# Attention with sinks and windows, then a leaky-ReLU MLP: sinks' loads, the order of the first copies, and GpSimd for the sinks of chunk 0

## The chip, the cores and the metric

The kernel runs on one core of a Trainium2 chip. Its engines are TensorE (PE), VectorE (DVE), ScalarE (ACT), GpSimd (POOL) and SyncE (SP); each runs its own instructions in order, and they wait for one another by semaphores. The metric is the device time of one execution in microseconds, lower is better.

## What is computed

Four batches of 8 heads, 768 positions, head size 64. Heads 0, 2 and 6 ("retrieval") attend to all earlier positions; heads 1, 3, 4, 5 and 7 ("streaming") only to the first 4 positions (the sinks) and to the last 64. The result, 3072 tokens of 512, goes through two matrices with a leaky ReLU between them.

```python
scores = scale * np.matmul(q, k.transpose(0, 1, 3, 2))
stream_keep = causal & (is_sink | in_win)
scores = np.where(mask, scores, -1e9)          # causal, or stream_keep for streaming heads
a = np.exp(scores - max); a = a / a.sum(-1)
x = (a @ v) as [B * S, H * D]
h = x @ w_in                                    # 512 -> 2048
g = np.maximum(0.01 * h, h)
out = g @ w_out                                 # 2048 -> 512
```

## The kernel before

The tokens are cut into 8 chunks of 384: chunk n is half c = n % 2 of batch b = n // 2. For each chunk the kernel brings q and k into the layout with the head size across the partitions (`qt`, `kt`), computes scores per head into PSUM, exponentiates them on ScalarE into `at` (retrieval) or `ats` (streaming), multiplies by v into the accumulator `po` of each pair of heads, divides by the sums (`finish`, L499 and L501, giving `xs`), transposes to `xt` (`x_t`, L512 and L515) and runs the MLP (L562 for w_in, L570 for the leaky ReLU, L602 for w_out). The order on each engine is that of the program text: nothing is reordered, and the program interleaves attention of one chunk with the MLP of another by hand (`slots`, `merge`).

Chunk 0 is special, since there is nothing to run beside it. Its k is loaded in float32 in two halves by SP (`load_k0`, tile `f`) and cast by DVE and ACT (`kb`, L312, L313). Its q is loaded and cast by one DMA of POOL (`load_q0`, L80). `prep_first` transposes both on TensorE (L324, L329) and empties the results from PSUM: `k_rows(half, hh)` (L341 on DVE, L339 on ACT) for heads 2p + hh of two pairs p, `q_rows(half)` (L355 on DVE, L357 on ACT). Filler matmuls (`warm_up`, L200) lie between. Two masks are added to the scores of chunk 0 by TensorE: `n_caus` (L423) and, for streaming heads, `n_win0` (L463), which `negative_window` (L178, L179) makes on DVE.

The sinks are handled apart. `sv` holds the first 4 rows of v of each head and batch (L650: five small DMAs on ACT's queue, one for each streaming head and all batches). `sink_values` (L187, L189) spreads them into `vs`, one column block to a head, with the 0/1 mask `m_h`; `sink_keys` (L238) copies the sinks' columns of `kt` into `ksink`; `sink` computes all sinks' scores at once (L396, then the exponential at L399), and `finish` adds `vs` times these to the accumulators. `sink_after` says after which heads the sinks' slot comes. `v_shift_pe` (L224, L227) makes `vb`, v moved by 64 rows, for the first two tiles; later chunks do it by DMA (`v_shift`, L215, L216).

POOL issues nearly all loads, in program order, each after the one eight before it has landed: for chunk 0 q, v (`va`, L97) and the first two quarters of w_in (L103), then k, q and v of chunk 1 (`kb`, `qb`, `va`), the other quarters of w_in and those of w_out (L106), and four memsets of `kz` (L674, L675). Chunk 1's k and q are transposed at L272, after the first seven groups of the MLP of chunk 0.

Of the kernel before, what the change touches and what calls it, by code (L numbers as in the profile page):

```python
# [13 lines left out]
ACTF = mybir.ActivationFunctionType  # L14
ALU = mybir.AluOpType

IS_RETR = [1, 0, 1, 0, 0, 0, 1, 0]
# [4 lines left out]
def kernel(  # L22
# [12 lines left out]
    nc = tc.nc  # L35
    B, H, S, D = q.shape
    assert (B, H, S, D) == (4, 8, 768, 64)
    NS = int(n_sink)
# [43 lines left out]
    def load(n, nms="kqv"):  # L82

        b, c = divmod(n, 2)
        for nm in nms:
            if nm == "k" and n >= BY_DMA:

                for g in range(3):
                    for hh in range(2):
                        nc.gpsimd.dma_start(out=kz[n % 2][:, g, hh::2, D * hh : D * hh + D],  # L90
                                            in_=nat[nm][b, c, :, hh::2, g])
                continue
            if nm != "v":
                cast[nm, n] = rot.tile([128, 3, H, D], BF16, name=f"{nm}b", tag=f"{nm}b", bufs=2)
            for g in range(3):
                o = va[b % 2][:, 3 * c + g, :, 0:D] if nm == "v" else cast[nm, n][:, g]
                nc.gpsimd.dma_start(out=o, in_=nat[nm][b, c, :, :, g])  # L97

    def load_w(which, i):

        if which == "in":
            c = slice(512 * i, 512 * i + 512)
            nc.gpsimd.dma_start(out=w_in_bf[:, :, c], in_=w_in_r[:, :, c])  # L103
        else:
            c = slice(4 * i, 4 * i + 4)
            nc.gpsimd.dma_start(out=w_out_bf[:, c, :], in_=w_out_r[:, c, :])  # L106
# [12 lines left out]
    kt = [bf(f"kt{i}", 4, 2, S) for i in range(2)]  # L119
    va = [bf(f"va{i}", 6, H, D + 1) for i in range(2)]  # L120
    vb = [bf(f"vb{i}", 5, H, D + 1) for i in range(2)]
    vs = [bf(f"vs{i}", H, D + 1) for i in range(2)]

    sv = one.tile([128, B, D], FP32, name="sv")
# [21 lines left out]
    m_h = bf("m_h", H)  # L146
# [9 lines left out]
    def spread(ap, n, w):  # L156
        return ap.rearrange("p (o r) -> p o r", o=1).to_broadcast([128, n, w])

    def shifts():

        nc.vector.tensor_copy(shift[:, 0, 0:64], ident[:, 64:128])
        nc.vector.tensor_copy(shift[:, 1, 64:128], ident[:, 0:64])

    def masks_sinks():

        with nc.allow_low_precision("one term of each sum is not zero"):
            nc.vector.tensor_reduce(m_h[:], ident[:, 0 : NS * H].rearrange("p (h r) -> p h r", r=NS),
                                    axis=mybir.AxisListType.X, op=ALU.add)
        for h in range(H):
            if IS_RETR[h]:  # L170
                nc.vector.memset(m_h[:, h : h + 1], 0.0)
# [11 lines left out]
        nc.vector.tensor_copy(m_win0[:, 0, :], m_caus[:, 0:64])  # L183
        nc.vector.memset(m_win0[0:NS, 1, :], 1.0)

    def sink_values(b):
        nc.vector.tensor_copy(vs[b % 2][:, :, D], m_h[:])  # L187
        m = m_h[:, 1:H].rearrange("p (h o) -> p h o", o=1).to_broadcast([128, H - 1, D])
        nc.vector.tensor_tensor(vs[b % 2][:, 1:H, 0:D], spread(sv[:, b, :], H - 1, D), m, op=ALU.mult)  # L189


    idle = {}
# [1 line left out]
    def warm_up(n, w=128):  # L194
        if not idle:
            idle["s"] = bf("idle", 512)
            nc.vector.memset(idle["s"][:], 0.0)
            idle["d"] = bank("psS", [128, 512], FP32)
        for _ in range(n):
            nc.tensor.matmul(idle["d"][:, 0:w], lhsT=idle["s"][:, 0:128], rhs=idle["s"][:, 0:w], start=True, stop=True)  # L200
# [9 lines left out]
    def v_shift(n, eng=None):  # L210
        eng = eng or nc.scalar
        b, c = divmod(n, 2)
        i = b % 2
        lo, hi = (0, 2) if c == 0 else (2, 5)
        eng.dma_start(out=vb[i][0:64, lo:hi], in_=va[i][64:128, lo:hi])  # L215
        eng.dma_start(out=vb[i][64:128, lo:hi], in_=va[i][0:64, lo + 1 : hi + 1])  # L216
# [9 lines left out]
            src = p[:, 0:w].rearrange("p (h d) -> p h d", h=7)  # L226
            nc.vector.tensor_copy(vb[0][:, t, 1:H, :], src)  # L227

    def sink_keys(n):
        b, c = divmod(n, 2)  # L230
        if c:
            return
        for hh in range(2):
            r = slice(64 * hh, 64 * hh + 64)
            d = ksink[b % 2].rearrange("p (a c) -> p a c", a=4)[r, :, NS * hh : NS * hh + NS]
            st = [p for p in range(4) if not IS_RETR[2 * p + hh]]
            for ps2 in [slice(0, 4)] if len(st) == 4 else [slice(p, p + 1) for p in st]:
                nc.vector.tensor_copy(d[:, ps2], kt[b % 2][r, ps2, hh, 0:NS])  # L238

    def prep_pair(n, p, tag="pt", eng=("v", "v", "v")):  # L240
        b, c = divmod(n, 2)
# [66 lines left out]
    def prep_first():  # L308

        k0 = stage["k"].rearrange("p h (g d) -> p g h d", g=3)  # L310
        qts[0] = rot.tile([128, 4, CH], BF16, name="qt", tag="qt", bufs=3)
        nc.vector.tensor_copy(cast["k", 0][:, :, 0:4], k0[:, :, 0:4])  # L312
        nc.scalar.activation(out=cast["k", 0][:, :, 4:8], in_=k0[:, :, 4:8], func=ACTF.Copy)  # L313
        pts = {}
        for nm, half, tag in (("k", 0, "pt"), ("k", 1, "py"), ("q", 0, "po"), ("q", 1, "po")):
            pt = pts[nm, half] = bank(tag, [128, 2, 4, 128], BF16)
            if nm == "q":
                continue
            if half == 1:
                warm_up(9)  # L320
            for e in range(2):
                p = 2 * half + e
                for g in range(3):
                    nc.tensor.transpose(pt[:, e, g, :], cast[nm, 0][:, g, 2 * p : 2 * p + 2, :], ident[:])  # L324
        warm_up(8)
        for p in range(4):
            for g in range(3):
                for hh in range(2):
                    nc.tensor.transpose(pts["q", p // 2][64 * hh : 64 * hh + 64, p % 2, g, :],  # L329
                                        cast["q", 0][:, 2 * p + hh, D * g : D * g + D], ident[:])  # L330
        tok = lambda ap: ap.rearrange("p e (t g) -> p e t g", g=3)

        def k_rows(half, hh, act=False):
            ps2 = slice(2 * half, 2 * half + 2)
            r = slice(64 * hh, 64 * hh + 64)
            src = pts["k", half][r, :, 0:3, :].rearrange("p e g t -> p e t g")
            dst = tok(kt[0][r, ps2, hh, 0:CH])
            if act:
                nc.scalar.activation(out=dst, in_=src, func=ACTF.Copy)  # L339
            else:  # L340
                nc.vector.tensor_copy(dst, src)  # L341

        def q_rows(half):
            return (tok(qts[0][:, 2 * half : 2 * half + 2, :]),
                    pts["q", half][:, :, 0:3, :].rearrange("p e g t -> p e t g"))

        nc.vector.tensor_sub(m_w[:], m_caus[:, 64:128], m_caus[:, 0:64])
        negative_causal()
        k_rows(0, 0)
        k_rows(0, 1)  # L350
        k_rows(1, 0, True)
        k_rows(1, 1, True)
        negative_window()
        d, r = q_rows(0)
        nc.vector.tensor_copy(d, r)  # L355
        d, r = q_rows(1)
        nc.scalar.activation(out=d, in_=r, func=ACTF.Copy)  # L357


    xts = {}  # L360
# [260 lines left out]
    def run(*lists):  # L621
        for l in lists:
            for f in l:
                f()
# [6 lines left out]
    def merge(ms, as_):  # L631

        r, done = [], 0
        for j, m in enumerate(ms):
            want = (j + 1) * len(as_) // len(ms)
            r += as_[done:want] + [m]
            done = want
        return r + as_[done:]
# [6 lines left out]
    make_identity(nc, ident)  # L645
    warm_up(9, 512)
    nc.vector.memset(sv[:], 0.0)
    for h in range(H):
        if not IS_RETR[h]:
            nc.scalar.dma_start(out=sv[NS * h : NS * h + NS], in_=v[:, h, 0:NS, :].rearrange("b r d -> r b d"))  # L650
    for t in va:
        nc.vector.memset(t[:, :, :, D], 1.0)
    nc.vector.memset(shift[:], 0.0)
# [3 lines left out]
    load(0, "v")  # L657
    load_w("in", 0)
    load_w("in", 1)
    load(1, "kq")  # L660
    load(1, "v")
    load_w("in", 2)
    load_w("in", 3)
    for j, a in enumerate(ats):
        if j < 2:
            nc.vector.memset(a[:, :, 1:3, :], 0.0)
        else:
            z = idle["s"][:, 0:CH].rearrange("p (a e t) -> p a e t", a=3, e=2)
            nc.scalar.activation(out=a[:, :, 1:3, :], in_=z, func=ACTF.Copy)
    masks_sinks()  # L670
    for i in range(4):
        load_w("out", i)
    for t in kz:
        nc.gpsimd.memset(t[:, :, 0::2, D:], 0.0)  # L674
        nc.gpsimd.memset(t[:, :, 1::2, 0:D], 0.0)  # L675
    prep_first()
    A0 = Attention(0, ("psS", "ph"), po_tags=("po", "po", "py", "po"))
    a0 = A0.slots(order=[0, 2, 1, 3, 4, 5, 6, 7], lag=lambda t: 4, XLAG=None, sink_after={0, 2})
    warm_up(8)
    run(a0[0:4])  # L680
    sink_keys(0)
    sink_values(0)
    shifts()
    run(a0[4:6])
    v_shift_pe()
    run(a0[6:14])
    i0 = in_first(0, ("ph", "psS", "ph", "psS"))
# [22 lines left out]
    a1 = A1.slots(order=[0, 2, 6, 1, 3, 4, 5, 7], lag=lambda t: max(2, 7 - t // 2))  # L710
    run(a1[0:11])
    v_shift(1, nc.sync)
    run(merge(in0[8:12], a1[11:16]))
    out0 = out_slots(0, ("po", "ph", "py"))
    run(merge(in0[12:16] + out0[0:3], spaced(a1[16:], 9)))
# [72 lines left out]
```

## Time and profile before

| | |
|---|---|
| median of 4 runs | 237.67 us (237.25 to 238.12) |
| the profiled execution | 238.12 us |
| its span, first to last instruction | 236.4 us |
| instructions | 5109 |
| granted TensorE clock | 0.999 of full speed |
| TensorE / ScalarE / VectorE / GpSimd busy | 226.0 / 129.4 / 89.1 / 77.8 us |
| HBM read, written | 27.28 MB, 6.29 MB |

The profiled execution is the slowest of the four. A profile line of the timeline gives start, length, engine, line of the source, operation, output and inputs with shapes, how often; in brackets stands how long the engine was idle before it, and what released it. Matmuls overlap: the length of one is longer than the distance to the next. A line of the chain of waits gives start, length, and what held the end of the program in that time. DMA issues on the engines count as busy on POOL, and the last figure of an issue line is the time from issue to landing.

### The profile page before, as it was taken

To read this page: it belongs to the slowest core of one execution; us is meant where nothing else is said; L and a number is where in the kernel's file an instruction comes from. 1 tells how busy PE (TensorE), PEld (TensorE's weight loads), DVE (VectorE), ACT (ScalarE), POOL (GpSimd) and SP (SyncE) were. 2 spreads that over 40 slices of the span, in tenths; PEclk is the share of its full clock that TensorE was granted. 3 is DMA by queue.
4 is the path that set the end of the run, shared out by engine and by line. 5 is a ranking of instruction groups with operands and counts; after the bars stand their busy time and mean duration, and the time that the engine had idled before them with its cause. 6 is when DMAs were issued, how large, how long until landed. Compare 5 with 4: busy or idle time off the path is not lost.

```text
span 236.4 us, 5109 instructions
## 1 busy us (share of the span) xinstructions
PE 226.0 (96%) x2039; PEld 138.9 (59%) x2064; DVE 89.1 (38%) x244; ACT 129.4 (55%) x282; POOL 77.8 (33%) x102
## 2 busy tenths in 40 slices
PE   6799999999999999999989999999999999999994
PEld 2686666555664677566546665566556665555553
DVE  7754478307762244054211451244212441111121
ACT  4787776661551798756347763556356763433300
POOL 7958932789762263345039200000000000000000
PEclk9999999999999999999999999999999999999999
DMA  7999999999999999999999998495210211111112
GB/s 164 173 183 163 219 222 188 150 127 166 149 130 235 171 182 146 181 137 173 147 173 164 118 170 144 111 136 145 80 44 0 65 45 52 44 44 44 47 44 89
DMA packets 110699, 30.54 MB, mean 129 GB/s; under 512 B 101460, under 2 KB 106836, under 8 KB 110676
## 3 DMA queue, kind: packets, MB, share of 16 engines
q0 software_dynamic: 74144, 13.24, 74.6%
q1 hardware_dynamic: 36432, 16.95, 39.0%
q8 instruction: 16, 0.26, 0.5%
q14 instruction: 7, 0.06, 0.1%
q10 hardware_dynamic: 100, 0.02, 0.0%
HBM read 27.28 MB, written 6.29 MB: 142 GB/s over the span
## 4 chain that ended last, share of the span: by engine, by line
PE 85%; DMA 7%; ACT 3%; DVE 2%; issue 1%; POOLq 0%; ACTq 0%
PE ph L562 26%; PE py L602 14%; PE pt L602 10%; PE po L383 7%; PE psS L562 6%; PE ph L602 4%; PE psS L416 4%; PE psS L602 4%; DMA xt<-xs 4%; DMA q<-in_q_dram 3%; PE psS L458 2%; ACT at L425 2%; PE po L602 1%; PE psS L396 1%; PE ph L416 1%
## 5 line engine op out<-in xcount | busy, mean ns | idle before, releaser
L562 PE MATMUL ph<-xt,w_in_bf 128*128 128x384 bf16 x416 | 85.7, 326 | 0.8 <-DMA xt<-xs 0.6
L570 ACT ACTIVATE g<-ph 128x384 bf16<-128x384 f32 x102 | 50.2, 492 | 51.6 <-PE ph L562 51.3
L562 PEld LDWEIGHTS <-w_in_bf 128*128 128x128 bf16 x512 | 46.5, 98 | 31.4 <-issue 0.5
L602 PEld LDWEIGHTS <-g 128*128 128x128 bf16 x400 | 35.8, 98 | 26.3
L602 PE MATMUL py<-w_out_bf,g 128*128 128x512 bf16 (+1 forms) x164 | 42.5, 368 | 0.6
L425 ACT ACTIVATE at<-psS 128x384 bf16<-128x384 f32 x66 | 32.4, 494 | 11.6 <-PE psS L416 10.2
L90 POOL DMA_DIRECT2D kz<-in_k_dram x30 | 22.4, 768 | 29.5 <-DMA qb<-in_q_dram 12.1
L602 PE MATMUL pt<-w_out_bf,g 128*128 128x512 bf16 x103 | 28.4, 379 | 0.5
L97 POOL DMA_DIRECT2D va<-in_v_dram x24 | 21.1, 896 | 8.1 <-DMA w_out_bf<-in_moe_w_out_dram 3.3
L97 POOL DMA_DIRECT2D qb<-in_q_dram x21 | 18.6, 893 | 13.7 <-DMA va<-in_v_dram 7.6
L416 PE MATMUL psS<-qt,kt 128*128 128x384 bf16 (+2 forms) x86 | 21.5, 288 | 0.2
L562 PE MATMUL psS<-xt,w_in_bf 128*128 128x384 bf16 x96 | 20.5, 326 | 0.0
L383 PE MATMUL po<-va,at 128*128 128x65 bf16 x237 | 19.5, 193 | 0.2 <-DVE at L433 0.2
L383 PEld LDWEIGHTS <-at 128*128 128x128 bf16 x252 | 15.9, 98 | 5.6 <-issue 0.6
L466 ACT ACTIVATE ats<-psS 128x384 bf16<-128x384 f32 x32 | 15.8, 493 | 4.9 <-PE psS L458 4.0
L607 DVE COPY o<-py 128x512 f32<-128x512 f32 (+1 forms) x11 | 7.3, 665 | 28.0 <-PE py L602 28.0
L501 DVE TENSOR_TENSOR xs<-po,linv 128x384 bf16<-128x384 f32 x30 | 16.7, 558 | 1.0
L416 PEld LDWEIGHTS <-kt 128*128 128x128 bf16 x108 | 10.2, 97 | 8.8 <-issue 1.7
L458 PEld LDWEIGHTS <-kt 128*128 128x128 bf16 x240 | 11.8, 98 | 5.5 <-issue 0.2
L433 DVE TENSOR_TENSOR at<-at,m_caus 128x128 bf16<-128x128 bf16 x21 | 4.7, 225 | 26.4 <-ACT at L425 26.4
L383 PEld LDWEIGHTS <-ats 128*128 128x128 bf16 x240 | 11.4, 97 | 3.8 <-DVE ats L476 0.6
L570 ACT ACTIVATE g<-psS 128x384 bf16<-128x384 f32 x22 | 10.8, 492 | 4.7 <-PE psS L562 4.6
(135 smaller groups left out, 241.0 us busy)
## 6 DMA issues: line engine op xcount, KB each, us to landing
out_dram<-o SPq DMA_DIRECT2D x23, 256.0 KB, 2.6
va<-in_v_dram POOLq DMA_DIRECT2D x24, 128.0 KB, 10.8
qb<-in_q_dram POOLq DMA_DIRECT2D x21, 128.0 KB, 10.3
w_in_bf<-in_moe_w_in_dram POOLq DMA_DIRECT2D x4, 512.0 KB, 9.6
w_out_bf<-in_moe_w_out_dram POOLq DMA_DIRECT2D x4, 512.0 KB, 15.7
kz<-in_k_dram POOLq DMA_DIRECT2D x30, 64.0 KB, 7.4
vb<-va SPq DMA_DIRECT2D x8, 195.0 KB, 6.5
vb<-va SPq DMA_DIRECT2D x6, 130.0 KB, 7.9
```

Of the source, the lines that this page charges most:

```text
L90: nc.gpsimd.dma_start(out=kz[n % 2][:, g, hh::2, D * hh : D * hh + D], in_=nat[nm][b, c, :, hh::2, g])
L97: nc.gpsimd.dma_start(out=o, in_=nat[nm][b, c, :, :, g])
L383: nc.tensor.matmul(o, lhsT=lhsT, rhs=rhs, start=first, stop=False, skip_group_check=True)
L416: nc.tensor.matmul(s[:, off : off + w], lhsT=kt[i][:, p, hh, 128 * kj : 128 * kj + 128], rhs=qts[n][:, p, lo:CH], start=(j == 0), stop=(j ...
L425: nc.scalar.activation(out=a[:, 0:off], in_=s[:, 0:off], func=ACTF.Exp, scale=SM)
L458: nc.tensor.matmul(s[:, 64 * m : 64 * m + 64], lhsT=kt[i][:, p, hh, k0 : k0 + 128], rhs=qts[n][:, p, 64 * m : 64 * m + 64], start=(m == 0) ...
L466: nc.scalar.activation(out=av_, in_=s[:, 0:CH].rearrange("p (j e f) -> p j e f", j=3, e=2), func=ACTF.Exp, scale=SM)
L501: nc.vector.tensor_tensor(xs[:], po[:, :, :, 0:D], linv.to_broadcast([128, 3, 2, D]), op=ALU.mult)
L562: nc.tensor.matmul(ph[:, 0:CH], lhsT=w_in_bf[:, g, 128 * t : 128 * t + 128], rhs=xts[n][:, g, :], start=(g == 0), stop=(g == KG - 1))
L570: nc.scalar.activation(out=gs[n][:, t, :], in_=ph[:, 0:CH], func=ACTF.Prelu, alpha=0.01)
L602: nc.tensor.matmul(py[n][:, 0 : c1 - c0], lhsT=gs[n][:, ng, 128 * tt : 128 * tt + 128], rhs=w_out_bf[:, ng, c0:c1], start=(ng == 0), stop= ...
L607: nc.vector.tensor_copy(o[:, 0 : c1 - c0], py[n][:, 0 : c1 - c0])
```

## The change

- `sv` is loaded by one DMA to a batch on SP's queue, all eight heads' sinks in one (`load_sinks`): batch 0 at the start, after the two loads of `f`; batches 1 to 3 after `v_shift(1)`. The retrieval heads' rows are now loaded too; `m_h` makes them zero.
- In `prep_first` the first `q_rows` stands before the second `k_rows` on DVE, and the second `q_rows` goes from ACT to DVE, behind `negative_window`.
- `sink_values(0)` and `sink_keys(0)` run on POOL, and stand before the loads of chunk 1 in POOL's queue; `prep_first` is called before these loads too.
- `shifts()` runs before `prep_first`; three of the five `ats` are cleared by DVE instead of two.
- The sinks' slot of chunk 0 comes after heads 0 to 3 instead of after heads 0 and 2; `v_shift_pe` stays behind slot 5, and so comes ahead of the sinks.
- The eight filler matmuls ahead of chunk 0's scores are gone.

```diff
+    def load_sinks(b):
+        nc.sync.dma_start(out=sv[0 : NS * H, b, :], in_=v[b, :, 0:NS, :])
+
-    def sink_values(b):
-        nc.vector.tensor_copy(vs[b % 2][:, :, D], m_h[:])
+    def sink_values(b, eng=None):
+        eng = eng or nc.vector
+        eng.tensor_copy(vs[b % 2][:, :, D], m_h[:])
...
-        nc.vector.tensor_tensor(vs[b % 2][:, 1:H, 0:D], spread(sv[:, b, :], H - 1, D), m, op=ALU.mult)
+        eng.tensor_tensor(vs[b % 2][:, 1:H, 0:D], spread(sv[:, b, :], H - 1, D), m, op=ALU.mult)
...
-    def sink_keys(n):
+    def sink_keys(n, eng=None):
...
-                nc.vector.tensor_copy(d[:, ps2], kt[b % 2][r, ps2, hh, 0:NS])
+                (eng or nc.vector).tensor_copy(d[:, ps2], kt[b % 2][r, ps2, hh, 0:NS])
...
         k_rows(0, 0)
+        nc.vector.tensor_copy(*q_rows(0))
         k_rows(0, 1)
         k_rows(1, 0, True)
         k_rows(1, 1, True)
         negative_window()
-        d, r = q_rows(0)
-        nc.vector.tensor_copy(d, r)
-        d, r = q_rows(1)
-        nc.scalar.activation(out=d, in_=r, func=ACTF.Copy)
+        nc.vector.tensor_copy(*q_rows(1))
...
     nc.vector.memset(sv[:], 0.0)
-    for h in range(H):
-        if not IS_RETR[h]:
-            nc.scalar.dma_start(out=sv[NS * h : NS * h + NS], in_=v[:, h, 0:NS, :].rearrange("b r d -> r b d"))
+    load_sinks(0)
...
     load_w("in", 1)
-    load(1, "kq")
-    load(1, "v")
-    load_w("in", 2)
-    load_w("in", 3)
     for j, a in enumerate(ats):
-        if j < 2:
+        if j < 3:
...
     masks_sinks()
+    shifts()
+    sink_values(0, nc.gpsimd)
+    prep_first()
+    sink_keys(0, nc.gpsimd)
+    load(1, "kq")
+    load(1, "v")
+    load_w("in", 2)
+    load_w("in", 3)
     for i in range(4):
         load_w("out", i)
...
-    prep_first()
     A0 = Attention(0, ("psS", "ph"), po_tags=("po", "po", "py", "po"))
-    a0 = A0.slots(order=[0, 2, 1, 3, 4, 5, 6, 7], lag=lambda t: 4, XLAG=None, sink_after={0, 2})
-    warm_up(8)
-    run(a0[0:4])
-    sink_keys(0)
-    sink_values(0)
-    shifts()
-    run(a0[4:6])
+    a0 = A0.slots(order=[0, 2, 1, 3, 4, 5, 6, 7], lag=lambda t: 4, XLAG=None, sink_after={0, 1, 2, 3})
+    run(a0[0:6])
     v_shift_pe()
...
     v_shift(1, nc.sync)
+    for b in range(1, B):
+        load_sinks(b)
```

## The prediction

> **What bounds the kernel now.** I read the page first (shares, slices), then the chain of waits, then the timeline of each engine up to 20 us, since the diff touches almost nothing later.
>
> ```profile
> PE 226.0 (96%) x2039; PEld 138.9 (59%) x2064; DVE 89.1 (38%) x244; ACT 129.4 (55%) x282; POOL 77.8 (33%) x102
> PE   6799999999999999999989999999999999999994
> PE 85%; DMA 7%; ACT 3%; DVE 2%; issue 1%; POOLq 0%; ACTq 0%
> ```
>
> TensorE is 96% busy and carries 85% of the chain; what it lacks lies in the first slices. The chain of waits up to 45 us says how it starts (start, length, what):
>
> ```profile
> 1.33 7.70 DMA q<-in_q_dram
> ...
> 9.07 0.55 PE po L329 x12
> ...
> 9.64 0.97 DVE qt L355
> ...
> 10.65 0.32 PE ph L416
> ```
>
> Chunk 0's q lands at 1.33 + 7.70 = 9.03. Twelve transposes and one VectorE copy later the scores begin, at 10.65; from there to 20 us the chain is TensorE alone. A change here is worth what it does to 10.65, plus the stalls that it puts between 10.65 and 20. The timeline of VectorE, then of TensorE:
>
> ```profile
> 6.28 1.94 DVE L341 COPY kt<-pt 64x768 bf16<-64x768 bf16 x2 [0.51 <-PE pt L324]
> 8.25 0.32 DVE L178 TENSOR_SCALAR n_win<-m_w 128x320 bf16<-128x320 bf16 x1
> 8.63 0.09 DVE L179 MEMSET n_win<- 4x32 uint32 x1
> 9.64 0.96 DVE L355 COPY qt<-po 128x768 bf16<-128x768 bf16 x1 [0.92 <-PE po L329]
> 10.51 0.36 DVE L238 COPY ksink<-kt 64x4 bf16<-64x4 bf16 x2
> ...
> 15.22 0.20 DVE L499 RECIPROCAL linv<-po 128x6 f32<-128x6 f32 x1 [0.87 <-PE po L383]
> 15.45 0.56 DVE L501 TENSOR_TENSOR xs<-po,linv 128x384 bf16<-128x384 f32 x1
> ```
>
> ```profile
> 11.63 0.60 PE L396 MATMUL ph<-qt,ksink 128*128 128x256 bf16 x4
> 12.07 0.26 PE L383 MATMUL po<-va,at 128*128 128x65 bf16 x3
> ...
> 16.44 0.33 PE L512 MATMUL pt<-ident,xs 128*128 128x128 bf16 x3
> ```
>
> To be seen: both k copies and the window mask fit before 8.72, in time in which VectorE would wait for q anyway (0.92 us is still left idle).
>
> GpSimd issues the loads of chunk 1 early (timeline), and they land ten us later (DMA issues of the stretch 9 to 10 us, last figure):
>
> ```profile
> 6.01 1.52 POOL L103 DMA_DIRECT2D w_in_bf<-in_moe_w_in_dram x2
> 7.48 2.71 POOL L97 DMA_DIRECT2D kb<-in_k_dram x3
> 10.49 2.71 POOL L97 DMA_DIRECT2D qb<-in_q_dram x3 [0.30 <-DMA va<-in_v_dram]
> kb<-in_k_dram POOLq DMA_DIRECT2D x2, 128.0 KB, 10.1
> ```
>
> [...] kb, issued at 7.48, lands at 17.5, after w_in, issued at 6.01 and 6.77, has landed at 14.1 and 16.7; its ten us are backlog.[...] the one-output MEMSET kz of 768 elements took 0.757 us[...].[...] The trace grants 1.00 in every stretch from 1 to 20 us, with gaps of at most 1.22 us.
>
> **The change, part by part.**
>
> 1. *Sinks' v.* ACT's five issues (1.50 to 3.43) go; its table load, at 3.47, starts some 2 us earlier and its cast of k (6.02) waits for the second half of f (1.29 + 4.3 = 5.6) instead: 0.4 us earlier, for nothing, since q is later. Does q land sooner? In the DMA view the sv queue holds 43 packets at 1.6% of 16 engines from 3 to 6 us and 57 at 2.2% from 6 to 9: 0.8 + 1.1 = 1.8 engine-us[...]; I take 0[...]. Below nothing: the new load is one more behind f on SP, 32 rows of 256 B; under 0.05. The three late loads go on SP behind vb (24.35, 26.18), where nothing follows for several us; sink values of batch 1 come tens of us later.
>
> 2. *Order on VectorE.* One more ats memset (0.21) and the two shift copies (0.09 apart) come before the k cast: 4.63 becomes 4.9 to 5.0, the first k copy ends near 7.65 instead of 7.25, hidden by q at 9.03. Then the first q copy at 9.64, as before: scores still at 10.65. Behind it now stand the second k copy (0.97): 10.52 to 11.49; mask (0.32) to 11.84; its memset to about 11.99; second q copy, from ACT, 11.95 to 12.95.
>
> 3. *Order on TensorE.* The fifth slot was the sinks' scores at 11.63; now it is head 1, whose k comes at 11.5 and whose bank is free at 11.06 + 0.49 = 11.55: no wait. Its six matmuls end at 11.80, then the mask matmul waits for the memset until 12.03: **+0.23**. The sinks' scores move behind v_shift_pe, to about 13.5; second q copy (12.95) is there. ACT has the exponentials in another order; each bank is freed in time.
>
> 4. *Finish.* Pairs 0 and 1 now finish together after the sinks' slot and h6's second score: the first reciprocal goes from 15.22 to about 15.86. Reciprocal and product take 15.45 - 15.22 + 0.56 = 0.79, so the first xs is ready at 16.65 and, with 0.05 to signal, its transposes at 16.70, where TensorE arrives at about 16.6: up to 0.1 more, of which the third part's wait already covers some. The next pairs follow at 0.71 and keep up (xs of pair 2 at 18.07 for 18.25, of pair 3 at 18.78 for 19.06). By my walk the first w_in matmul goes from 17.35 to 17.60: **+0.25** for parts 3 and 4 together.
>
> 5. *GpSimd.* After 7.5: vs copy (0.15, as a small memset), product of 448 elements[...], 0.44 by the memset's rate; I take 1.0, to 2 with overhead. Then it waits for the second k copy (11.5), copies, and is free at about 11.9. Sink keys are needed at 13.5: 1.6 spare; vs at 15.6. **0**. Everything queued behind goes late: kb from 7.48 to 11.9 (to 14.6), qb to 17.3, va to 20.0, the third w_in from 18.69 to about 20. But kb's turn in the DMA queue only comes at 16.7, qb's at 19.4, va's at 22.2, w_in's at 26.2: each is issued 2 us or more ahead, so landings stay (kb 19.4 for its transposes at 21.92; third w_in 28.1 for 29.86): **0**. The cover is 2.5 us and 1.7; if it goes, the rival below.
>
> 6. *The eight filler matmuls* (9.86 to 10.48) lay in a wait; removing them leaves a gap of 0.7 us[...]: **0**[...].
>
> Sum: +0.25 on the profiled execution, 238.12 to 238.37; that one is the slowest of four, so on the median 237.67 + 0.25 = **237.9**.
>
> **Rivals.**
>
> - *q lands sooner.* If the sv loads are what holds q's last packets, or these come sooner for another reason, 9.03 could become about 8.1; then transposes, copy and scores follow directly. Bounded by the fillers in front of the q transposes (end near 8.2) and by va's landings (10.2 to 11.9), 0.5 to 1.3 less the 0.25: 236.6 to 237.4, I say 237.0. For: q is first in the chain. Against: 1.8 engine-us of sv.
> - *Slower: the loads of chunk 1 keep their ten us.* If time to land goes with the issue and not with the backlog, kb's third load lands at 13.7 + 10.1 = 23.8 instead of 19.4, and TensorE, at its second kb transposes near 23.2 and qb's at 24.6 (last qb 16.4 + 9.9 = 26.3), waits about 1.7: 239.6. It decides once kb lands later than about 22.2. For: 4.4 us of delay is more than the 2.5 of cover. Against: first-in first-out order of the landings.
> - *The change does nothing that shows*: the mask's wait is absorbed by a later wait (0.64 us for xt at 123.5): 237.7. It is counted with the forecast.
>
> **How the numbers follow.** About 0.3% (0.7 us) is what a measurement here tells from no change. Forecast with its absorbed variant 0.60 (237.4 to 238.4); q sooner 0.20; loads late 0.10; a fallen clock or a GpSimd slower than I think 0.10 (238.6 to 240). Of "q sooner" 0.14 falls beyond -0.7 us and the rest within; of the slower cases nearly all beyond, plus 0.03 of the forecast's tail: faster 0.15, same 0.62, slower 0.23. The range 236.6 to 238.9 leaves out about 0.05 below and 0.15 above.
>
> **What would show it.** Right: q's landing near 9.0; score at 10.65; a wait of 0.2 us of the first n_win matmul on the memset; GpSimd's idle time up to 11.5 and kb issued near 12 yet landing before 20; first w_in matmul near 17.6. Wrong: q before 8.5, kb after 22, a granted clock under 1.00 before 15 us, or sinks' scores waiting for GpSimd.

## The result, and the profile after

The kernel after takes 238.60 us in the median of 43 executions (236.46 to 240.3); the kernel before 237.34 us (236.43 to 239.34, 64 executions). The ratio is 1.0049 with a 95% interval of 1.0034 to 1.0065: slower, by about 1.2 us. The profiled execution of after took 239.32 us with a span of 237.6, against 236.4 for the span of before. First the page of after, its engines' busy time and its shares of the chain of waits.

```profile
PE 226.3 (95%) x2031; PEld 138.6 (58%) x2056; DVE 88.8 (37%) x242; ACT 128.4 (54%) x280; POOL 79.4 (33%) x106
PE 84%; DMA 7%; DVE 3%; ACT 3%; issue 1%; POOLq 0%; ACTq 0%
```

TensorE's work has not grown; VectorE holds 1% more of the chain. The chain of waits of after up to 20 us shows where (start, length, what held the end):

```profile
1.32 8.23 DMA q<-in_q_dram
...
9.59 0.55 PE po L334 x12
...
10.16 0.96 DVE qt L355
11.12 0.03 issue
11.15 0.97 DVE kt L346
...
12.14 0.33 DVE n_win L178
...
12.52 0.10 DVE n_win L179
...
12.66 0.32 PE ph L466
...
16.52 0.21 DVE linv L502
...
16.75 0.56 DVE xs L504
17.31 0.11 DVE linv L502
...
17.46 0.25 PE po L386 x3
```

Before, VectorE left this chain at 10.61 and did not come back before 20 us; now it holds it in two stretches more, 11.15 to 12.62 and 16.52 to 17.42. With the starts of three TensorE steps in both profiles the whole of the 1.2 us can be put in its place:

| start, us | before | after | added by then |
|---|---|---|---|
| q's transposes | 9.07 | 9.59 | 0.52 |
| first score | 10.65 | 11.17 | 0.52 |
| first w_in matmul | 17.35 | 18.46 | 1.11 |
| from there to the end of the span | 219.05 | 219.14 | 1.20 in all |

Three terms make up the 1.11. q lands 0.52 later. TensorE then has the six matmuls ahead of the first `n_win` matmul behind it at about 12.34 (they start at 12.17, and six take 0.17), and waits 0.32 for the mask's memset, 12.52 + 0.10. And the finish holds it once: TensorE is through with pair 2 near 17.19 (its last two matmuls start at 17.08) and needs an accumulator bank that VectorE gives back only when it has divided pair 0 (16.75 + 0.56) and taken the second reciprocal; it goes on at 17.46, 0.27 later. 0.52 + 0.32 + 0.27 = 1.11. Only the last two, 0.59 together, can be laid to the change from this pair of profiles: q landed at 7.4 to 9.8 us in the profiles of kernels that load it alike, as is shown below, so the 0.52 may be chance.

GpSimd's part is what the prediction expected. Its timeline in after (start, length, work, idle time and its releaser):

```profile
8.11 0.93 POOL L194 TENSOR_TENSOR vs<-sv,m_h 128x448 bf16<-128x448 f32 x1 [0.34 <-DMA sv<-in_v_dram]
8.99 0.18 POOL L243 COPY ksink<-kt 64x4 bf16<-64x4 bf16 x1
12.27 0.19 POOL L243 COPY ksink<-kt 64x16 bf16<-64x16 bf16 x1 [3.10 <-DVE kt L346]
12.74 2.71 POOL L97 DMA_DIRECT2D kb<-in_k_dram  x3 [0.27 <-issue]
```

It stands 3.10 us for the second k copy, and the loads of chunk 1 go out at 12.74 instead of 7.48. From issue to landing they now take about half, as the DMA issues of after up to 20 us say (last figure; before: 10.1 and 9.9):

```profile
kb<-in_k_dram POOLq DMA_DIRECT2D x3, 128.0 KB, 5.3
qb<-in_q_dram POOLq DMA_DIRECT2D x3, 128.0 KB, 5.4
```

So they land at about the same time as before, and TensorE's waits after 20 us have none for them.

A single profile is not enough here, because executions of one and the same kernel differ by 2 us: before, a third of them lie below 237.0, the others up to 239.3. The profiles of this study, one to a kernel, show two terms that differ among kernels that issue them alike. One is q's landing, 7.4 to 9.8 us. The other is a wait at about 123 us, for a transposing DMA of `xt`; the waits of TensorE after 20 us, first in before, then in after (total, times, longest):

```profile
PE ph L562 <- DMA xt<-xs: 0.6, 1, 0.6
```

```profile
PE ph L565 <- DMA xt<-xs: 0.7, 1, 0.7
```

In the other profiles it is between 0 and 1.2. Take it from the rest of the span and what is left is 218.4 in before (219.05 - 0.64) and 218.4 in after (219.14 - 0.7): nothing past 20 us has changed. An effect of a few tenths must therefore be read from the mean of many executions, and a profile tells only its place. Most experiments have 14 to 22 executions, which leaves 0.1 to 0.25 us of standard error on a mean; before's own mean over all 237 of its executions, those beside the experiments taken in, is 237.36 (237.31 to 237.50 in the groups).

### The profile page after: what moved, and what is told of

Same layout as the page of the kernel before. It is cut to its first block, busy times and chain, and to the rows that moved or that the text cites. A ratio compares the mean times of both kernels' runs of the same rounds, so it can differ in the third digit from the quotient of the medians.

```text
span 237.6 us, 5088 instructions
## 1 busy us (share of the span) xinstructions
PE 226.3 (95%) x2031; PEld 138.6 (58%) x2056; DVE 88.8 (37%) x242; ACT 128.4 (54%) x280; POOL 79.4 (33%) x106
## 4 chain that ended last, share of the span: by engine, by line
PE 84%; DMA 7%; DVE 3%; ACT 3%; issue 1%; POOLq 0%; ACTq 0%
PE ph L565 26%; PE py L605 13%; PE pt L605 10%; PE po L386 7%; PE psS L565 6%; PE ph L605 4%; PE psS L419 4%; PE psS L605 4%; DMA xt<-xs 4%; DMA q<-in_q_dram 3%; PE psS L461 2%; ACT at L428 2%; PE po L605 1%; PE psS L399 1%; PE ph L419 1%
```

## The experiments

### 1. The fillers back

After, with the eight filler matmuls where before has them:

```diff
+    warm_up(8)
     run(a0[0:6])
```

> The changed kernel with the eight filler matmuls back ahead of chunk 0's scores. Theory 'order' (two waits of TensorE that the new order makes, 0.32 us for the window mask and 0.27 us for the accumulator's bank, in every execution): both waits stay, the time is 0.6 us above before. Theory 'clock' (without the fillers the granted clock falls for a stretch in some executions: 10 of 44 of the changed kernel were at 0.990 to 0.993, all over 239.3 us): no execution under 0.997, the mean some 0.4 us below the changed kernel's 238.5, and none of the group at 239.4 to 239.8. Theory 'sv' (the new load holds back q's last packets): as the changed kernel, 238.5.

Measured: median 238.09 us, ratio 1.0024 (1.0002 to 1.0047), mean 237.92 of 22 executions, against 238.54 for after. So about 0.6 (standard error 0.27) of the 1.2 us hangs on the fillers. The granted clock of all executions accounts for a part: of 44 of after (the profiled one is among them), nine, not ten as the expectation has it, have a mean clock of 0.990 to 0.993, and these average 239.65 us, the rest 238.25. With the fillers it was one of 22. That makes about 0.2 of the 0.6. The other executions also differ, 238.25 against 237.85, by 0.4 with a standard error of 0.3; no run here explains that, and it may be chance.

### 2. The fillers alone taken from before

```diff
-    warm_up(8)
     run(a0[0:4])
```

> The kernel before without the eight filler matmuls ahead of chunk 0's scores, nothing else. Theory 'clock': a quarter of the executions at a granted clock of 0.990 to 0.993 and about 1.6 us longer, the mean 0.4 us above before (237.3). Theories 'order' and 'sv': no change, 237.3 within 0.2 us, all clocks at 0.997 or more.

Measured: median 237.45, ratio 1.0022 (1.0003 to 1.0041), mean 237.62. Three of 22 executions have a clock of 0.991 and stand at 238.9 to 239.4; the others average 237.38, as before does. So in this kernel the fillers' removal costs nothing in most executions and 1.5 to 2 us in some. With the fillers, 7 of 173 executions of before whose clock is on record fell in the same way.

### 3. After with the old order of the copies

After, with `k_rows(0, 1)`, the other k copies, `negative_window` and then both `q_rows` as before has them:

```diff
     k_rows(0, 0)
-    nc.vector.tensor_copy(*q_rows(0))
     k_rows(0, 1)
...
     negative_window()
-    nc.vector.tensor_copy(*q_rows(1))
+    d, r = q_rows(0)
+    nc.vector.tensor_copy(d, r)
+    d, r = q_rows(1)
+    nc.scalar.activation(out=d, in_=r, func=ACTF.Copy)
```

> The changed kernel with the copies of k and q in the order and on the engines of before (both k copies and the mask ahead of the first q copy on VectorE, the second q copy on ScalarE); all else as changed. Theory 'order': the 0.32 us wait for the mask goes, the 0.27 us wait for the bank (it comes from the later sinks' slot) stays; 0.3 us faster than the changed kernel, about 238.2. Theories 'clock' and 'sv': as the changed kernel, 238.5, with low clocks in a quarter of the executions.

Measured: median 237.79, ratio 1.0023 (0.9996 to 1.005), mean 238.11; four of 22 executions at a clock of 0.990 to 0.993. The profile caught one of these. Its table by stretches (length, busy time of PE, PEld, DVE, ACT and POOL with instructions, then PEclk, DMA share, GB/s):

```profile
8.00:10.00 2.00, 0.20 (x8) 0.20 (x10) 0.71 (x3) 0.81 (x2) 1.29 (x4) 1.00 2.17 162
10.00:12.00 2.00, 1.28 (x28) 0.98 (x23) 0.96 (x1) 0.81 (x1) 2.00 (x3) 0.80 1.38 201
12.00:14.00 2.00, 2.00 (x19) 1.59 (x18) 0.00 (x0) 1.90 (x4) 2.00 (x3) 0.50 1.26 209
14.00:16.00 2.00, 2.00 (x24) 1.44 (x22) 0.65 (x2) 0.98 (x2) 2.00 (x3) 0.84 1.84 175
```

and the TensorE timeline around it:

```profile
9.80 0.86 PE L334 MATMUL po<-ident,q 128*64 128x128 bf16 x24 [2.19 <-DMA q<-in_q_dram]
11.38 0.48 PE L421 MATMUL ph<-qt,kt 128*128 128x384 bf16 x1 [0.72 <-DVE qt L360]
```

The clock is at half from about 11.2 to 14.6 us: the scores run at 0.48 us instead of 0.32, and the first w_in matmul comes 8.51 us after the first score instead of 6.70. This is the fallen clock that the prediction had among its rivals, with 0.10 for it and a slower GpSimd together. The profiled execution of after has nearly the same two gaps, 2.00 and 0.72, and kept its clock. So with nearly the same gaps one execution fell and one did not; of all, four of 22 fell here and nine of 44 in after.

### 4. The new load of the sinks' v alone

Before, with `load_sinks(0)` in place of the five loads on ACT, and the later batches' after `v_shift(1)`:

```diff
-    for h in range(H):
-        if not IS_RETR[h]:
-            nc.scalar.dma_start(out=sv[NS * h : NS * h + NS], in_=v[:, h, 0:NS, :].rearrange("b r d -> r b d"))
+    load_sinks(0)
...
     v_shift(1, nc.sync)
+    for b in range(1, B):
+        load_sinks(b)
```

> The kernel before with the changed loads of the sinks' v alone: one on SP at the start, three late. Theory 'sv': q lands some 0.5 us later than at 9.03 and the time is 0.4 to 0.5 us above before. Theories 'order' and 'clock': q lands within 0.2 us of 9.0, the time is that of before, 237.3 within 0.2 us.

Measured: median 237.91, ratio 1.0034 (1.0018 to 1.005), mean 237.84. The new loads are not free, they cost about half a microsecond. The edit moves one more thing: without its five issues ScalarE begins its table load at 0.81 us instead of 3.47. In the profile q landed 7.9 us after its issue, hardly later than before's 7.7, so the trace of this one execution doesn't show where the time goes.

### 5. The order alone

Experiment 1 with the five old loads of the sinks' v in place of all `load_sinks`. What remains of the change is the order on VectorE, the sinks' later slot, GpSimd's work and the late loads of chunk 1.

> The changed kernel with the sinks' v loaded as before (five small DMAs on ScalarE's queue) and the eight filler matmuls back: of the change there remain the order of the copies, the later sinks' slot and GpSimd's part. Theory 'order': 0.6 us above before in executions where q lands near 9 or later; where q lands near 7.5 the first score comes some 0.5 us earlier than before can have it, since before copies all of k first, and the two cancel; on the mean +0.1 to +0.5, 237.5 to 237.9. Theory 'sv' alone: 237.3, as before. Low clocks (under 0.996) as seldom as before, 3 of 75.

Measured: median 237.76, ratio 1.0013 (0.9989 to 1.0037), mean 237.68 of 14 executions, 0.3 above before (standard error 0.2). The profile caught an execution with q early. Its TensorE timeline (start, length, work):

```profile
7.57 0.86 PE L334 MATMUL po<-ident,q 128*64 128x128 bf16 x24
9.14 0.32 PE L419 MATMUL ph<-qt,kt 128*128 128x384 bf16 x1 [0.17 <-DVE qt L355]
```

The first w_in matmul comes at 16.44, 7.30 after the first score.

### 6. The new loads and GpSimd, without the order

Experiment 3 with the sinks' slot after heads 0 and 2 again, and the fillers:

```diff
-    a0 = A0.slots(order=[0, 2, 1, 3, 4, 5, 6, 7], lag=lambda t: 4, XLAG=None, sink_after={0, 1, 2, 3})
+    a0 = A0.slots(order=[0, 2, 1, 3, 4, 5, 6, 7], lag=lambda t: 4, XLAG=None, sink_after={0, 2})
+    warm_up(8)
```

> The changed kernel with the copy order, the sinks' slot and the fillers of before: of the change there remain the sv loads on SP and the work and waits of GpSimd with the later loads of chunk 1. Theory 'sv' (new load costs 0.5 us): 237.8, as the run with the new sv loads alone (mean 237.84). Theory that the later loads of chunk 1 or GpSimd cost something: above 238.2, and in the trace TensorE waits for kb, qb or w_in after 20 us. Theory 'order': 237.3.

Measured: median 237.87, ratio 1.0024 (1.0009 to 1.004), mean 237.81. That is experiment 4 again (237.84), though here GpSimd makes the sinks' keys and values and the loads of chunk 1 go out late. So these two parts of the change cost nothing that shows. The loads start at 9.41 us here and at 12.74 in after, though; that they are in time even from there is shown by after's own profile alone. This profile too has q early:

```profile
7.52 0.86 PE L334 MATMUL po<-ident,q 128*64 128x128 bf16 x24
9.83 0.32 PE L421 MATMUL ph<-qt,kt 128*128 128x384 bf16 x1 [0.89 <-DVE qt L360]
```

Beside experiment 5 it gives the price of the order, both ways. With q at 7.5 the old order holds the first score until 9.83, since VectorE first makes both k copies and the mask; the new one has it at 9.14, 0.69 sooner. From first score to first w_in matmul it is 6.70 here and 7.30 there, so the new order gives 0.60 back: w_in at 16.53 and 16.44, a tie. With q at 9 or later, VectorE has done the k copies in the old order (by 8.22 in before), nothing is won, and the 0.60 is lost whole.

### 7. GpSimd's next loads later

To see whether GpSimd's issuing of the next loads holds q up (the theory 'descriptors' below), the kernel before with its four memsets of `kz` ahead of the loads of v, so that GpSimd starts no DMA between q's and 6.1 us:

```diff
     mask_causal()
+    for t in kz:
+        nc.gpsimd.memset(t[:, :, 0::2, D:], 0.0)
+        nc.gpsimd.memset(t[:, :, 1::2, 0:D], 0.0)
     load(0, "v")
```

> The kernel before with GpSimd's four kz memsets (3 us) moved up, between the masks and the loads of v[...]; v, w_in and all later loads are issued 3 us later. The time is set by when q lands, and that varies by 2 us[...]. Theory 'descriptors'[...]: q lands at 7.5 to 7.8 in the trace, the mean falls to about 236.7 and the spread to under 1 us. Theory 'not descriptors': q's landing keeps its spread from 7.5 to 10, the mean stays at 237.3 or rises by what the later loads cost.

Measured: median 239.41, ratio 1.0091 (1.0058 to 1.0123). q landed 6.5 us after its issue, which other executions also reach. The profile's span, 237.9, is 1.5 above before's, for two reasons. VectorE's cast of k took 2.06 us instead of 1.05, so that the transposes of k and, behind them, those of q came late, and the first w_in matmul at 18.10 instead of 17.35. And the late loads of chunk 1 now hold the chain. The chain of waits of this kernel, and below it TensorE's timeline:

```profile
11.94 11.39 DMA kb<-in_k_dram
```

```profile
11.40 0.32 PE L416 MATMUL ph<-qt,kt 128*128 128x384 bf16 x1 [0.17 <-DVE qt L355]
...
23.37 0.40 PE L272 MATMUL py<-ident,kb 128*128 128x128 bf16 x4 [0.42 <-DMA kb<-in_k_dram]
```

Here `kb`, issued from 10.20 on, did keep its eleven us and TensorE did wait: v and w_in had been issued late as well, from 6.09 and 8.72 on (3.38 and 6.01 in before), the first w_in landed at 17.07, and `kb`'s turn came behind them. So the rival "the loads of chunk 1 keep their ten us" names something real. In after it did not come about because v and w_in had gone out at 3.4 to 7.5 us and were through when `kb`'s turn came: w_in's second load landed at 17.2, `kb`'s first at 18.05. Whether GpSimd's issues hold q stays open: it is one trace, and the moved memsets had the other effect too.

### 8. The small load behind q

Experiment 4, with batch 0's small load on SP only after the second quarter of w_in has been issued, at 8 us, so that it cannot lie beside most of q, which landed at 9.3 in the profile (its memset goes to GpSimd):

```diff
-    load_sinks(0)
...
     load_w("in", 1)
+    load_sinks(0)
```

> The kernel before with the sinks' v of batch 0 loaded by one DMA on SP, but only after 7.5 us (its clearing memset moves to GpSimd, behind the second w_in issue), the others late: no sv packet is in the DMA engines while most of q goes through. Theory 'sv' (the new load's packets[...] hold q's last packets back): the 0.5 us of the run with the new loads alone is gone, mean 237.3 or less. Rival (the cost is not from packets beside q's, but from the later small loads or from the queue): still 237.8.

Measured: median 239.46, ratio 1.0114 (1.008 to 1.0149), six executions. The cover was gone: in the chain of waits the small load now stands itself.

```profile
7.97 5.77 DMA sv<-in_v_dram
...
13.85 0.63 DVE vs L193
14.47 0.10 DVE shift L161
```

8 KB took 5.77 us, beside v and w_in. VectorE stood 1.88 us for it, and behind VectorE the shift matmuls. In five of six executions the clock fell as well, and in the profile it did so before VectorE's wait (TensorE's timeline, then the stretches, in the form of experiment 3):

```profile
9.39 1.43 PE L333 MATMUL po<-ident,q 128*64 128x128 bf16 x24 [2.00 <-DMA q<-in_q_dram]
```

```profile
8.00:10.00 2.00, 0.60 (x14) 0.61 (x16) 0.34 (x2) 0.62 (x1) 2.00 (x3) 0.87 2.08 166
10.00:12.00 2.00, 2.00 (x26) 1.66 (x23) 1.68 (x4) 0.81 (x1) 1.60 (x3) 0.50 1.31 197
12.00:14.00 2.00, 2.00 (x26) 1.71 (x25) 0.15 (x1) 1.70 (x5) 1.53 (x2) 0.77 1.25 207
```

TensorE stood once, 2.00 us for q, and the clock is at half from about 9.5 to 12.9. The fillers have their place behind q's transposes and start at 10.76 here, when the clock has fallen. The experiment thus says nothing of q, which it was made for; it says what the load's early place is worth.

### 9. The small load by GpSimd

Experiment 4, with batch 0's load as a DMA of GpSimd between q's and v's:

```diff
     mask_causal()
+    load_sinks(0, nc.gpsimd)
     load(0, "v")
```

> The kernel before with the sinks' v of batch 0 loaded by one DMA on GpSimd's queue, right behind q's and ahead of v's, the other batches late on SP: no sv packet of another queue runs beside q's. Theory 'sv' (the one load on SP[...] costs 0.5 us): mean back at 237.3 or below, since nothing of another queue is beside q any more. Rival (the 0.5 us of the run with the new loads alone comes from what else that run changed, the three late loads or ScalarE's earlier start): still 237.8.

Measured: median 237.77, ratio 1.0028 (1.0002 to 1.0054), mean 238.02 of 14 executions. The cost is still there when the load comes behind q in GpSimd's own queue, which speaks against its place on SP as the cause. It is less certain here: three of the 14 executions have a fallen clock, and the others average 237.58.

### 10. Both orders' good halves

The first q copy ahead of the k copies only as far as it wins something: mask first, then q, and the second k copies on ScalarE; sinks after heads 0 and 2; old loads, fillers, GpSimd as in after. In place of after's lines:

```diff
     k_rows(0, 0)
+    negative_window()
     nc.vector.tensor_copy(*q_rows(0))
-    k_rows(0, 1)
+    k_rows(0, 1, True)
     k_rows(1, 0, True)
     k_rows(1, 1, True)
-    negative_window()
     nc.vector.tensor_copy(*q_rows(1))
```

> The changed kernel with the sv loads and the fillers of before, the sinks' slot again after heads 0 and 2, and the copies in a third order: VectorE makes the first k copy, the mask, both q copies; ScalarE makes the second k copy and the two others, ahead of q's landing. Theory 'order' (what costs is the mask's wait and the later sinks' slot, what gains is that the first q copy need not wait for all of k): first w_in matmul 6.7 us after the first score, as before, with the first score 1.6 us behind q's landing however early that is; mean 0.2 to 0.4 us below before. If the theory is wrong and GpSimd's part costs: above before.

Measured: median 237.39, ratio 0.9993 (0.9976 to 1.001), mean 237.22. Its TensorE timeline:

```profile
9.17 0.86 PE L334 MATMUL po<-ident,q 128*64 128x128 bf16 x24 [1.42 <-DMA q<-in_q_dram]
10.75 0.32 PE L419 MATMUL ph<-qt,kt 128*128 128x384 bf16 x1 [0.17 <-DVE qt L356]
```

The first w_in matmul follows at 17.45, 6.70 after the first score: the 0.60 of after's order is gone, though q's first rows still come ahead. The whole is 0.14 us below before, which cannot be told from none; the gain that an early q should bring (0.69 in a third of the executions, some 0.2 on the mean) is within what this run leaves open. It is the best kernel of the study and not shown to beat the one before.

### 11. The late loads alone

Before, with the five small loads of ACT cut to batch 0, and batches 1 to 3 loaded late as after does:

```diff
-            nc.scalar.dma_start(out=sv[NS * h : NS * h + NS], in_=v[:, h, 0:NS, :].rearrange("b r d -> r b d"))
+            nc.scalar.dma_start(out=sv[NS * h : NS * h + NS, 0], in_=v[0, h, 0:NS, :])
...
     v_shift(1, nc.sync)
+    for b in range(1, B):
+        load_sinks(b)
```

> The kernel before with batch 0's sink values by the five loads on ACT as they were, now of that batch alone, and the later batches' by three small loads on SP behind vb, as after has them. It takes the change of the sinks' v apart: e4, which has the whole of it, stood at +0.45 us. If the cost of e4 is the late loads (three DMAs on SP in the stretch of batch 0's chunk 1, or what queues behind them), this run shows it too: ratio near 1.002, mean 0.4 to 0.5 us above before. If the cost is in the one new load (its 32 rows, its place on SP, ACT's earlier table load and cast), this run is at before, 0 within 0.25 us, or up to 0.1 below, since less of sv moves beside q.

Measured: median 237.15, ratio 0.9984 (0.9959 to 1.001), mean 237.30 of 14 executions, 5 of them below 237.0, as large a part as of before's. The late loads cost nothing that shows.

### 12. The 32-row form on ACT

Before, with four loads of 32 rows, one to a batch, on ACT in place of its five:

```diff
-    for h in range(H):
-        if not IS_RETR[h]:
-            nc.scalar.dma_start(out=sv[NS * h : NS * h + NS], in_=v[:, h, 0:NS, :].rearrange("b r d -> r b d"))
+    for i in range(B):
+        nc.scalar.dma_start(out=sv[0 : NS * H, i, :], in_=v[i, :, 0:NS, :])
```

> The kernel before with four loads of 32 rows on ACT, one to a batch, all at the start in place of the five by head; no late loads, nothing new on SP, ACT with nearly as many issues as before (four, not five). If it is the form of the load (32 rows of 256 B[...]) that delays q, this run has it four times over: mean 0.4 us or more above before, ratio 1.002 or more, q's landing at 9 us or later in the profile. If the form is harmless and the place (on SP, ACT free earlier) or the late loads do it, this run is at before, 0 within 0.25 us. If neither this run nor the one with the late loads alone shows a cost, what is left is the load's place behind f on SP or ACT's earlier table load and cast of k.

Measured: median 238.08, ratio 1.0027 (1.0 to 1.0055), mean 238.19 of 14 executions, and none of them under 237.6; five lie at 237.60 to 237.63. This run has a cause of its own, which the profile shows. Four loads of 32 rows hold ScalarE for 3.39 us, where the five of before hold it for 1.93, and its cast of k, behind them in its program, comes 1.46 later. ScalarE and TensorE in this run, and then in before:

```profile
1.50 3.39 ACTq L649 DMA_DIRECT2D sv<-in_v_dram  x4
...
7.48 0.83 ACT L313 ACTIVATE kb<-f 128x768 bf16<-128x768 f32 x1
...
8.36 0.51 PE L324 MATMUL py<-ident,kb 128*128 128x128 bf16 x6 [1.21 <-ACT kb L313]
...
9.24 0.86 PE L329 MATMUL po<-ident,q 128*64 128x128 bf16 x24
```

```profile
1.50 1.93 ACTq L650 DMA_DIRECT2D sv<-in_v_dram  x5
...
6.02 0.83 ACT L313 ACTIVATE kb<-f 128x768 bf16<-128x768 f32 x1
...
6.90 0.51 PE L324 MATMUL py<-ident,kb 128*128 128x128 bf16 x6 [0.15 <-ACT kb L313]
```

TensorE takes q's transposes behind those of k, so here they cannot start before 9.24, however early q lands; in this execution q was in time and they follow without a wait. So the first score comes at 10.82 at the soonest, where the old order with an early q has it at 9.83 (experiments 6 and 9), and 0.99 more than before's fastest execution, 236.41, is 237.4: this alone keeps the run from the early executions of before. The run therefore doesn't tell whether 32 rows in one load cost anything by themselves. The wait for `xt`, after 20 us, was also long in this profile:

```profile
PE ph L562 <- DMA xt<-xs: 1.2, 1, 1.2
```

What can be said of the new loads is this. The late ones are at before (11). With the early one, on SP (4 and 6) or on GpSimd's queue (9), all three with the old order and the fillers, the mean is 237.87 of 58 executions (standard error 0.10), 0.51 above before, and 5 of 58 lie below 237.0 where a third of before's do. Experiment 1 has the load as well, under the new order, and doesn't bear this out: 7 of its 22 lie below 237.0, and it is 0.24 (standard error 0.29) above experiment 5, its like with the old loads. By what way the early load costs stays open. In all three kernels ScalarE also starts earlier, and no run here parts the two. The landings of q in their profiles (7.9, 6.1 and 6.3 us from the issue) are hardly later than in before, and the wait for `xt` at 123 us was 0, 0.5 and 1.1 in them against 0.6 in before and 0 in 5, 10 and 11. Three profiles cannot tell a shift of such a term from chance.

## Why the prediction was right and where it was wrong

It said 237.9 with a range of 236.6 to 238.9, and 0.62 for no difference that can be told. The time, 238.6, lies in the range; the sign of the sum was right and its size wrong: +0.25 on the profiled execution against +1.2. The outcome, slower by more than 0.3%, had 0.23. That the time falls within the range is partly luck: the base, 237.67 from four executions, was 0.3 above the median of 64, and with that median the same sum gives 237.6, a full microsecond too little. By its own parts:

1. *Sinks' v*, "I take 0" for q's gain, below nothing "under 0.05". Wrong in sign: the kernels with the new load stand about 0.5 above before on the mean (experiments 4, 6 and 9). The bound below nothing was reckoned from the few packets of the load alone; what else the load moves, or delays, stays open. The working also took q's 9.03 for a property of the kernel, and in the profiles q's landing has a range of 2.4 us. That the late loads hurt nobody was right (11).
2. *Order on VectorE.* The step assumed that the second k copy starts while the q copy drains, 10.52 for 9.64. It did not: after's copy started at 11.15, at the very end of 10.16 + 0.96, 0.99 behind the start of the other instead of 0.88. In before the instruction behind the q copy started at 10.51, 0.87 behind it. What held the copy in after, no run shows.
3. *Order on TensorE*, "+0.23": a wait at that place, of 0.32. The mechanism was right, 0.09 too small because of that copy.
4. *Finish*, "up to 0.1 more": 0.27. This is the term that was mis-sized. I followed only the xs transposes, and found TensorE about as late as they. What TensorE waits for is ahead of them: the accumulation of the last pair into a bank of `po` that pair 0 still holds. That its reader on VectorE goes from 15.22 to about 15.86, plus q's shift, was in the working; who else waits for that reader was not asked. Parts 3 and 4 together are 0.59 in after, and 0.60 in experiment 5, instead of 0.25. (In the profile of experiment 1 they come to 0.77: q was early there, and TensorE stood at 11.4 for the last of v as well.)
5. *GpSimd* 0, and the loads of chunk 1 0: right. 0.93 us for the product where 1.0 had been taken; an idle time until the second k copy; `kb` at 12.74 for "near 12", its last load landed at 19.9. Experiment 6 equals experiment 4. The rival "loads late" fell in after, and experiment 7 shows the case in which it would have held.
6. *The filler matmuls* 0, for "a gap of 0.7 us": wrong. The 0 was an estimate that the profile of before did not show. I looked at the one gap of 0.7, and left out that it follows on the 2.0 for q with only 0.86 us of transposes between. In the kernels without fillers (after, 2 and 3) 16 of 88 executions have a mean clock of 0.990 to 0.993; in the kernels 1, 4, 5, 6 and 9 to 12, which have them, 8 of 144, and in before 7 of 173. (Experiments 7 and 8, whose starts differ more, have 1 of 7 and 5 of 6.) The profiles show a fall at 11.2, behind a gap of 2.19 us and within the next, of 0.72 (experiment 3), and one behind a single gap of 2.00 (experiment 8, which has the fillers); after kept its clock with 2.00 and 0.72. What decides it is not shown. In the two profiles that have a fall the half clock lasts about 3.4 us. Its price was 1.4 us in after (nine executions at 239.65, the others at 238.25). The fall's chance of 0.10 was meant for the kernel as a whole, where it is a share of the executions, and so belongs in the sum: some 0.3 us in after, 9 of 44 times 1.4, of which before has 0.1 too (7 of 173 times 2.1).

Taken each from the runs that part it best, the three are about 0.5 for the load, 0.3 for the order (0.6 less what an early q wins; experiment 5) and 0.2 for the clock, each uncertain by 0.1 to 0.2: together 1.0, where 1.2 was measured. The split is not pinned down further. Experiment 1, with load and order together, is only 0.56 above before instead of 0.8, and after is 0.62 above experiment 1, where the clock explains 0.2. That the pair of profiles also gives 1.2 may be chance, since 0.52 of it is q's landing.

## What to carry to other kernels

Where the start of a kernel hangs on one large load, look at several executions before a few tenths are argued from one, and ask of a new order how it stands for an early and for a late landing: here the copy moved ahead won 0.69 us with the input there early, and what was pushed behind it cost 0.60 early or late. When an instruction on VectorE becomes later, follow every reader of the banks that it releases, not only of the tile that it writes. Matmuls that fill a wait may be keeping the clock (here it fell in 16 of 88 executions without them and in 8 of 144 with them): look at all gaps around them, not at the one they stand in alone, and at the clock of many executions, since it fell in some only. When small loads are put on an engine that computes, look at how long issuing them holds it (1.93 and 3.39 us of ScalarE here), and at what stands behind them in its program.

## What the runs showed of the hardware that was not expected

- q's one load of 384 KB took 6.1 to 8.4 us from issue to landing in profiles of kernels that issue it at the same time and in the same way, and a transposing DMA at 123 us kept TensorE for 0 to 1.2 us. Their ranges are wide enough for the 2 us between executions of one kernel.
- Issuing four loads of 32 rows held ScalarE for 3.39 us, 0.85 each; five loads of 16 rows (4 rows for each of 4 batches) held it for 1.93, 0.39 each (experiment 12 and before). The early load of 32 rows went with half a microsecond on the mean (237.87 against 237.36) on SP or on GpSimd's queue. Why is not known.
- TensorE's clock fell to half for about 3.4 us after a single gap of 2.00 us (experiment 8), and kept full speed with gaps of 2.00 and 0.72 in another execution of another kernel (after).
- 8 KB issued at 7.97 us on SP's queue, beside v and w_in on GpSimd's, took 5.77 us.
- VectorE's cast of half of k took 2.06 us (experiment 7) in a stretch with GpSimd's memsets of `kz`:

```profile
4.63 2.06 DVE L312 CAST kb<-f 128x768 bf16<-128x768 f32 x1
```

  In before it took 1.05 and in after 0.73, where GpSimd was issuing DMAs in that stretch. It was not tried further.
